# A 32- or 64-row tail of a mixture-of-experts layer on separate column groups of the matrix engine, its sums added up by VectorE

## The chip, the cores and the metric

The kernel runs on one core of a Trainium2 chip. The metric is the device time of one execution in microseconds (us). A core has a matrix engine (PE, with PEld for its weight loads), VectorE (DVE), ScalarE (ACT), GpSimd (POOL) and a sequencer that issues DMAs (SP). PE holds a block of weights of up to 128 rows by 128 columns and streams a second operand past it; the sums land in PSUM, a small memory of eight banks per partition. DVE and ACT read PSUM and write SBUF, and each of the engines runs its own instructions in the order in which they are written.

## What is computed

A causal linear attention over 4 x 768 tokens makes a matrix x of 3072 tokens by 512. Each token then goes to its two best of 8 experts:

```
for e in range(E):
    for k in range(2):
        mask = top2[:, k] == e
        h = np.maximum(x[mask] @ w1[e], 0.0)
        out[mask] += top2_w[mask, k, None] * (h @ w2[e])
```

w1[e] is 512 x 1024 and w2[e] is 1024 x 512. Inputs and outputs are float32. The kernel keeps both operands of a product as a high and a low half in float16 and adds three products (high x high, high x low, low x high).

## The kernel before

The first 230 us are the attention, the gate and the routing, with expert 0 (e = 0) begun as lists of tokens come in. From there the program does one expert after another, e = 1 to 7, and the same engines work ahead on the next expert's weights and tokens.

An expert has tiles of 128 tokens: `tiles(e)` is 7 where the expert has a tail, else 6. `TAILS = (64, 64, 32, 32, 32, 0, 0, 0)` are the rows of the last tile (t = 6) of e = 0 to 7; from e = 1 on the experts are taken in order of how many tokens they have. So there are five tail tiles in the program, two of 64 rows and three of 32.

The first layer (`gemm1`, line 944, with `mm1` and `evac1`) goes by part: the seven tiles are one part of four tiles (512 columns) and one of two tiles and the tail (288 or 320 columns), or 256 columns where there is no tail. For each of 8 blocks f of the hidden size PE makes 12 products into one of four PSUM banks named `pS` (line 955); ACT then writes the high half of the hidden values `ht` (line 961), and DVE the low half (line 965), in two instructions where the part holds a tail. PE can start a fifth block only when DVE has read the first one's bank.

The second layer (`gemm2`, line 988) goes by tile: 24 products of 512 columns into one of two banks `pO` and `pKV` in turn (line 1000), then on DVE one `scalar_tensor_tensor` that scales by the token's gate weight and adds the rows `pv` gathered from the output so far (line 1012), then a scatter by POOL (line 1019). For e = 0 the scaled rows go to `PV[t]` (line 1015).

The tail had a path of its own (lines 1003 to 1011): the high and the low half of `ht` for its n rows lie side by side, so that 16 products with weights of 2n columns give high x high and high x low in rows 0 to n and low x high in rows n to 2n. ACT copies rows n to 2n out of PSUM (line 1008), DVE adds rows 0 to n (line 1009), and the line 1012 or 1015 follows.

The order is written out by hand. In an expert's second layer, behind each tile's `gemm2`, stand the steps for the next expert (lines 1327 to 1343): the scale and split of its first-layer weights (`split_w`, lines 861 and 862), and `trans_rows` for one of its tiles, which is on DVE a block transpose `turned` (line 924), on ACT `xth` (926), on DVE `xtl` (927) and four small ones (929). Behind the tail tile of e = 1, 2 and 3 stands one more `trans_rows`; behind that of e = 4 none, since e = 5 has six tiles. Next come the `gemm1` blocks of the next expert's first part: 288 columns for e + 1 = 2, 3, 4, and 256 for e + 1 = 5.

Of the kernel before, what the change touches and what calls it, by code (L numbers as in the profile page):

```python
# [26 lines left out]
AF = mybir.ActivationFunctionType  # L27
# [12 lines left out]
FB = F // 128  # L40
# [9 lines left out]
FULL = (NT - 1) * TS  # L50
# [44 lines left out]
def size(e, t):  # L95
    return TS if t < NT - 1 else TAILS[e]
# [35 lines left out]
def kernel(  # L132
# [3 lines left out]
    nc = tc.nc  # L136
    MULT, ADD, SUB = OP.mult, OP.add, OP.subtract
# [67 lines left out]
    for i in range(7):  # L205
        n = 1 << i
# [510 lines left out]
    for hp in range(HP):  # L717
        nc.tensor.matmul(PO[0][0][half(side(0, hp)), hp, :], SA[0, 1][half(0), hp, :], qTs[0][half(0), hp, C:],
                         start=True, stop=True)
# [29 lines left out]
    W2 = [[wp.tile([128, 2, DM], HF, name=f"w2{n}{f}") for f in range(FB // 2)] for n in "hl"]  # L749
# [10 lines left out]
    WS, REC, RECQ, PV, HT = {}, {}, {}, [], []  # L760
# [109 lines left out]
    def part_of(t):  # L870

        return min(i for i in range(NG) if t < sum(PARTS0[:i + 1]))
# [95 lines left out]
    def ht(e, part, f, c):  # L968

        at = c.start + (0 if not part else TAILS[e] if c.start >= FULL else LOW)  # L970
        return HT[0][:, f, at:at + c.stop - c.start]
# [3 lines left out]
    winv0 = consts.tile([128, NG], FT, name="winv0")  # L975
# [13 lines left out]
    def gemm2(e, t, then={}):  # L989
        n = size(e, t)  # L990
        cs = slice(t * TS, t * TS + n)
        p = psum.tile([128, DM], FT, name=("pO", "pKV")[next(turn) % 2])
        terms = [(f, a, b) for f in range(FB) for a, b in ((0, 0), (0, 1), (1, 0))]
        o = hp.tile([TS, DM], FT, name="ot", bufs=2) if e else PV[t]
        w, pv = WR[e % 2][:n, t:t + 1], PV[t][:n, :]
        if n == TS:
            for i, (f, a, b) in enumerate(terms):
                if i in then:
                    then[i]()
                nc.tensor.matmul(p, ht(e, a, f, cs), W2[b][f // 2][:, f % 2, :], start=(i == 0),  # L1000
                                 stop=(i == len(terms) - 1))
        else:
            for i in range(2 * FB):
                f, b = i // 2, i % 2
                nc.tensor.matmul(p[:2 * n, :], HT[0][:, f, FULL:FULL + 2 * n], W2[b][f // 2][:, f % 2, :],  # L1005
                                 start=(i == 0), stop=(i == 2 * FB - 1))
            o = o[:n, :]
            nc.scalar.activation(o, p[n:2 * n, :], AF.Copy)
            nc.vector.tensor_add(o, o, p[:n, :])
            p = o  # L1010
        if e:
            nc.vector.scalar_tensor_tensor(o, p, w, pv, op0=MULT, op1=ADD)  # L1012
            scatter_out(e, t, o)
        else:
            nc.vector.tensor_scalar(o, p, w, winv0[:n, part_of(t):part_of(t) + 1], op0=MULT, op1=MULT)

    def scatter_out(e, t, o):
        nc.gpsimd.memset(spacer, 0.0)
        st = nc.gpsimd.indirect_dma_start(  # L1019
            out=out, out_offset=bass.IndirectOffsetOnAxis(ap=REC[e, t], axis=0), in_=o, in_offset=None,  # L1020
            bounds_check=NTOK - 1, oob_is_err=False)
        if t == 0:
            out_st.clear()
        for s in out_st:
            tc.declare_no_dep(st.ins, s.ins, reason="an expert has a token once")
        out_st.append(st)
# [21 lines left out]
    for t in range(NST):  # L1048
# [45 lines left out]
        if 2 * t in GB[1:]:  # L1094
            b = GB.index(2 * t) - 1
# [69 lines left out]
    for i, (t0, n) in enumerate(parts(0)):  # L1165
# [51 lines left out]
        for t in range(t0, t0 + n):  # L1217
            gemm2(0, t, then.get(t, {}))
            if t == 0:
                finish(2, "gated")  # L1220
            if t == 1:
                advance(FILLG)
            if i == 2:
                scatter_out(0, t, PV[t][:size(0, t), :])
            if i == 2:
                if t == t0:
                    scale_w(1, 1)
                for j in range((0, 2, 3)[t - t0], (2, 3, 4)[t - t0]):
                    split_w(1, 1, j)
                for j in range((0, 2, 4)[t - t0], (2, 4, 4)[t - t0]):  # L1230
                    square_w(2, 1, j)
                if t == NT - 1:
                    scale_w(2, 1)
                for j in X1[t]:
                    trans_rows(1, j)
# [62 lines left out]
    for e in range(1, E):  # L1298
# [28 lines left out]
        for t in range(tiles(e)):  # L1327
            gemm2(e, t)
            if e == 1:
                next(ovj, None)  # L1330
            if e + 1 < E:
                if not t:
                    scale_w(1, e + 1)
                elif t < 5:
                    split_w(1, e + 1, t - 1)
                    square_w(2, e + 1, t - 1)
                elif t == 5:
                    scale_w(2, e + 1)
                for j in nxt[t:t + 1]:
                    trans_rows(e + 1, j)  # L1340
                    gather_pieces(2)
                    if e + 2 < E and j < tiles(e + 2):
                        gather_rows(e + 2, j)
    with tc.For_i(0, n_over) as it:
# [34 lines left out]
        for f in range(FB):  # L1379
            p = psum.tile([128, OV], FT, name="pS", bufs=4)  # L1380
            for d in range(DB):
                for i, (a, b) in enumerate(((0, 0), (0, 1), (1, 0))):
                    nc.tensor.matmul(p, W1[a][d][:, f * 128:(f + 1) * 128], xt(b, slice(0, OV))[:, d],
                                     start=(d == 0 and i == 0), stop=(d == DB - 1 and i == 2))
# [3 lines left out]
        p = psum.tile([OV, DM], FT, name="pO")  # L1388
        for f in range(FB):
            for i, (a, b) in enumerate(((0, 0), (0, 1), (1, 0))):  # L1390
                nc.tensor.matmul(p, ht(0, a, f, slice(0, OV)), W2[b][f // 2][:, f % 2, :],
                                 start=(f == 0 and i == 0), stop=(f == FB - 1 and i == 2))
        o = hp.tile([OV, DM], FT, name="ot", bufs=2)
# [30 lines left out]
```

## Time and profile before

| | |
|---|---|
| median of 3 runs | 703.85 us (702.4 to 705.42) |
| the profiled execution | 701.57 us, of which the span of its instructions 699.8 us |
| granted clock of PE, mean over the span | 0.99 |
| PE, DVE, ACT, POOL busy | 673.0, 419.1, 310.4, 361.5 us |

The busy time of an engine says how much it does over the whole span. What a change at one place is worth is read at that place: the timeline there gives for each instruction its start and length, and in brackets how long its engine sat idle before it and what ended that.

### The profile page before, as it was taken

To read this page: it belongs to the slowest core of one execution; us is meant where nothing else is said; L and a number is where in the kernel's file an instruction comes from. 1 tells how busy PE (TensorE), PEld (TensorE's weight loads), DVE (VectorE), ACT (ScalarE), POOL (GpSimd) and SP (SyncE) were. 2 spreads that over 40 slices of the span, in tenths; PEclk is the share of its full clock that TensorE was granted. 3 is DMA by queue.
4 is the path that set the end of the run, shared out by engine and by line. 5 is a ranking of instruction groups with operands and counts; after the bars stand their busy time and mean duration, and the time that the engine had idled before them with its cause. 6 is when DMAs were issued, how large, how long until landed. Compare 5 with 4: busy or idle time off the path is not lost.

```text
span 699.8 us, 15988 instructions
## 1 busy us (share of the span) xinstructions
PE 673.0 (96%) x6033; PEld 403.2 (58%) x6033; DVE 419.1 (60%) x1147; ACT 310.4 (44%) x533; POOL 361.5 (52%) x504
## 2 busy tenths in 40 slices
PE   7899999989989999999999999999999999999994
PEld 5788888775655464464446444644564474456441
DVE  4744988989646656782567257626743782576210
ACT  2267667771127653454335433534353544335100
POOL 4412343313333586578777857775774668331221
PEclk9999999999999999999999999999999999999997
DMA  9999986582383652644355435533462454211110
GB/s 201 238 264 229 259 238 198 186 293 73 99 272 136 188 171 77 183 131 135 118 170 161 115 102 170 161 111 117 134 194 82 146 161 152 69 46 38 59 50 36
DMA packets 94193, 104.33 MB, mean 149 GB/s; under 512 B 41234, under 2 KB 66844, under 8 KB 94112
## 3 DMA queue, kind: packets, MB, share of 16 engines
q1 hardware_dynamic: 79456, 65.73, 33.1%
q0 software_dynamic: 13552, 37.00, 16.8%
q10 hardware_dynamic: 1104, 0.53, 0.5%
q8 instruction: 49, 0.80, 0.5%
q14 instruction: 32, 0.26, 0.1%
HBM read 78.28 MB, written 26.12 MB: 149 GB/s over the span
## 4 chain that ended last, share of the span: by engine, by line
PE 71%; DVE 14%; issue 6%; DMA 4%; ACT 2%; POOL 1%; ACTq 0%; SPq 0%; POOLq 0%; DVEq 0%
PE pS L955 32%; PE pO L1000 13%; PE pKV L1000 12%; PE pO L398 2%; PE pS L386 2%; PE pS L342 2%; DVE at L389 2%; DVE w1l L862 1%; PE pS L464 1%; PE pS L433 1%; PE pS L358 1%; PE pKV L398 1%; DMA xg<-x_tok,recs 1%; PE pO L1005 1%; DMA Mk<-powd 1%
## 5 line engine op out<-in xcount | busy, mean ns | idle before, releaser
L1000 PEld LDWEIGHTS <-ht 128*128 128x128 f16 x1152 | 112.3, 98 | 134.2 <-issue 1.0
L897 POOL DMA_INDIRECT xg<-x_tok,recq x147 | 160.5, 1092 | 44.8 <-issue 41.5
L955 PE MATMUL pS<-xth,w1h 128*128 128x512 f16 (+3 forms) x544 | 175.5, 323 | 3.3 <-DVE ht L965 3.3
L955 PE MATMUL pS<-xtl,w1h 128*128 128x512 f16 (+3 forms) x544 | 175.3, 322 | 1.1 <-DVE wr L942 1.1
L955 PE MATMUL pS<-xth,w1l 128*128 128x512 f16 (+3 forms) x544 | 175.3, 322 | 0.3 <-DVE w1l L862 0.3
L955 PEld LDWEIGHTS <-w1h 128*128 128x128 f16 x1088 | 105.7, 98 | 71.5 <-issue 4.9
L965 DVE SCALAR_TENSOR_TENSOR ht<-pS,ht 128x256 f16<-128x256 f32 (+3 forms) x176 | 74.7, 453 | 105.8 <-ACT ht L961 103.8
L961 ACT ACTIVATE ht<-pS 128x512 f16<-128x512 f32 (+3 forms) x136 | 64.9, 482 | 128.6 <-PE pS L955 118.7
L1000 PE MATMUL pKV<-w2h,ht 128*128 128x512 f16 x384 | 119.1, 381 | 0.0
L1000 PE MATMUL pO<-w2h,ht 128*128 128x512 f16 x384 | 118.1, 379 | 0.0
L1019 POOL DMA_INDIRECT out_dram<-ot,rec x46 | 61.7, 1342 | 102.8 <-DVE ot L1012 71.9
L926 ACT ACTIVATE xth<-turned,xsc 128x512 f16<-128x512 f32 (+1 forms) x39 | 27.2, 697 | 132.1 <-DVE turned L924 132.1
L955 PEld LDWEIGHTS <-w1l 128*128 128x128 f16 x544 | 53.3, 98 | 35.0 <-issue 1.2
L1000 PE MATMUL pKV<-w2l,ht 128*128 128x512 f16 x192 | 73.3, 382 | 0.0
L1000 PE MATMUL pO<-w2l,ht 128*128 128x512 f16 x192 | 72.8, 379 | 0.0
L844 ACT ACTIVATE junk<-wst 128x1024 bf16<-128x1024 f32 x64 | 67.0, 1047 | 0.1
L374 POOL TENSOR_TENSOR kd<-kt,Mk 128x512 f32<-128x512 f32 x24 | 24.8, 1051 | 75.4 <-PE pR L433 52.1
L984 POOL DMA_INDIRECT pv<-out_dram,rec x46 | 46.7, 1015 | 12.8 <-issue 10.2
L927 DVE SCALAR_TENSOR_TENSOR xtl<-turned,xsc,xth 128x512 f16<-128x512 f32 (+1 forms) x39 | 28.2, 722 | 29.9 <-ACT xth L926 29.9
L862 DVE SCALAR_TENSOR_TENSOR w2l<-wst,wsc,w2h 128x1024 f16<-128x1024 f32 x32 | 40.9, 1281 | 4.5 <-ACT w2h L861 4.4
L389 DVE TENSOR_TENSOR at<-pS,Mk 128x512 f32<-128x512 f32 x48 | 29.8, 682 | 22.6 <-PE pS L386 18.1
L862 DVE SCALAR_TENSOR_TENSOR w1l<-wst,wsc,w1h 128x1024 f16<-128x1024 f32 x32 | 40.8, 1276 | 1.2 <-ACT w1h L861 1.2
(255 smaller groups left out, 893.3 us busy)
## 6 DMA issues: line engine op xcount, KB each, us to landing
wst<-in_moe_w_dram SPq DMA_DIRECT2D x36, 512.0 KB, 4.6
wst<-in_moe_w_dram SPq DMA_DIRECT2D x96, 128.0 KB, 2.8
x_tok<-xc SPq DMA_DIRECT2D x24, 272.0 KB, 4.6
kt<-in_k_dram SPq DMA_DIRECT2D x12, 512.0 KB, 4.7
qt<-in_q_dram SPq DMA_DIRECT2D x24, 256.0 KB, 5.4
vt<-in_v_dram SPq DMA_DIRECT2D x12, 512.0 KB, 5.4
out_dram<-zero SPq DMA_DIRECT2D x24, 256.0 KB, 3.2
xg<-x_tok,recq POOLq DMA_INDIRECT x147, 3.3
```

What stands on the lines that cost most here:

```text
L389: nc.vector.tensor_mul(at[:, s], ps[s], mask(s, slice(2 * r, 2 * r + 2), slice(0, C)))
L844: nc.scalar.activation(junk, WS[which, e, j], AF.Square, accum_out=wsq[:, which - 1, j:j + 1])
L862: nc.vector.scalar_tensor_tensor(lo[:, r], st[:, r], s, hi[:, r], op0=MULT, op1=SUB)
L897: nc.gpsimd.indirect_dma_start(out=XG[t][:, g * QW:(g + 1) * QW], out_offset=None, in_=x_tok.rearrange("t (q w) -> (t q) w", w=QW), in_off ...
L926: nc.scalar.activation(hi, raw, AF.Copy, scale=xs)
L927: nc.vector.scalar_tensor_tensor(lo, raw, xs, hi, op0=MULT, op1=SUB)
L955: nc.tensor.matmul(p, W1[a][d][:, fs], xt(b, cs)[:, d], start=(d == 0 and i == 0), stop=(d == DB - 1 and i == 2))
L961: nc.scalar.activation(ht(e, 0, f, cs), p, AF.Relu)
L965: nc.vector.scalar_tensor_tensor(ht(e, 1, f, c), p[:, r], 0.0, ht(e, 0, f, c), op0=OP.max, op1=SUB)
L984: nc.gpsimd.indirect_dma_start(out=PV[t][:size(e, t), :], out_offset=None, in_=out, in_offset=bass.IndirectOffsetOnAxis(ap=REC[e, t], axis=0),
L1000: nc.tensor.matmul(p, ht(e, a, f, cs), W2[b][f // 2][:, f % 2, :], start=(i == 0), stop=(i == len(terms) - 1))
L1019: st = nc.gpsimd.indirect_dma_start(out=out, out_offset=bass.IndirectOffsetOnAxis(ap=REC[e, t], axis=0), in_=o, in_offset=None, bounds_che ...
```

## The change

All 24 products of a tail are now made as for a whole tile, but each has weights of n columns only, and they go in turn to k = 128 / n separate places: product i writes PSUM partitions g n to (g + 1) n with g = i mod k. For 32 rows these are four groups of columns of the array, for 64 rows two. The k partial sums are then added: the first by the instruction that also scales and adds `pv`, each further one by another `scalar_tensor_tensor` on DVE that reads its PSUM rows, scales them and adds the output rows so far. The copy by ACT is gone. For e = 0, which has no `pv`, the gate weight is first scaled in place (a 64x1 instruction), the first sum is a `tensor_scalar`, the second a `scalar_tensor_tensor`.

```diff
-        else:
-            for i in range(2 * FB):
-                f, b = i // 2, i % 2
-                nc.tensor.matmul(p[:2 * n, :], HT[0][:, f, FULL:FULL + 2 * n], W2[b][f // 2][:, f % 2, :],
-                                 start=(i == 0), stop=(i == 2 * FB - 1))
-            o = o[:n, :]
-            nc.scalar.activation(o, p[n:2 * n, :], AF.Copy)
-            nc.vector.tensor_add(o, o, p[:n, :])
-            p = o
...
+        k = 128 // n
+        for i, (f, a, b) in enumerate(terms):
+            g = i % k
+            nc.tensor.matmul(p[g * n:(g + 1) * n, :], ht(e, a, f, slice(FULL, FULL + n)), W2[b][f // 2][:, f % 2, :],
+                             start=(i < k), stop=(i >= len(terms) - k))
+        o = o[:n, :]
+        if e:
+            nc.vector.scalar_tensor_tensor(o, p[:n, :], w, pv, op0=MULT, op1=ADD)
         else:
+            nc.vector.tensor_scalar(w, w, winv0[:n, part_of(t):part_of(t) + 1], None, op0=MULT)
+            nc.vector.tensor_scalar(o, p[:n, :], w, None, op0=MULT)
+        for g in range(1, k):
+            nc.vector.scalar_tensor_tensor(o, p[g * n:(g + 1) * n, :], w, o, op0=MULT, op1=ADD)
         if e:
-            nc.vector.scalar_tensor_tensor(o, p, w, pv, op0=MULT, op1=ADD)
             scatter_out(e, t, o)
```

On DVE at the tail of e = 2, between the two `trans_rows` that stand there (`turned`, `xtl` and `w` are theirs) and the first low halves `ht` of the next expert, the program before has:

```order
L929 SCALAR_TENSOR_TENSOR w_544<-rank,xg_2970 32x7 x4
L1009 TENSOR_TENSOR ot<-ot,pO 32x512
L1012 SCALAR_TENSOR_TENSOR ot<-ot,wr_541,pv_2979 32x512
L924 STREAM_TRANSPOSE turned<-xg_2972 128x512
L927 SCALAR_TENSOR_TENSOR xtl_532<-turned,xsc,xth_531 128x4x128
L929 SCALAR_TENSOR_TENSOR w_544<-rank,xg_2972 32x7 x4
L965 SCALAR_TENSOR_TENSOR ht<-pS,ht 128x256
```

and now, in the same place:

```order
L929 SCALAR_TENSOR_TENSOR w_544<-rank,xg_2970 32x7 x4
L1015 SCALAR_TENSOR_TENSOR ot<-pO,wr_541,pv_2979 32x512
L1020 SCALAR_TENSOR_TENSOR ot<-pO,wr_541,ot 32x512 x3
L924 STREAM_TRANSPOSE turned<-xg_2972 128x512
L927 SCALAR_TENSOR_TENSOR xtl_532<-turned,xsc,xth_531 128x4x128
L929 SCALAR_TENSOR_TENSOR w_544<-rank,xg_2972 32x7 x4
L965 SCALAR_TENSOR_TENSOR ht<-pS,ht 128x256
```

Two instructions of 512 elements became four, at the same point of DVE's order; e = 3 has the same picture. At the tail of e = 0, on DVE, the difference (`w1l` is the low half of the next expert's first-layer weights) is:

```order
 L939 SCALAR_TENSOR_TENSOR w_544<-rank,xg_2974 128x7
-L1009 TENSOR_TENSOR pv_2979<-pv_2979,pO 64x512
-L1015 TENSOR_SCALAR pv_2979<-pv_2979,wr_541,winv_557 64x512
+L1017 TENSOR_SCALAR wr_541<-wr_541,winv_557 64x1
+L1018 TENSOR_SCALAR pv_2979<-pO,wr_541 64x512
+L1020 SCALAR_TENSOR_TENSOR pv_2979<-pO,wr_541,pv_2979 64x512
 L862 SCALAR_TENSOR_TENSOR w1l_522<-wst,wsc,w1h_518 128x1024
```

Two instructions became three here, ahead of the split of the last weight block. At the tail of e = 4, on DVE, where no `trans_rows` follows, the difference is:

```order
 L929 SCALAR_TENSOR_TENSOR w_544<-rank,xg_2972 32x7 x4
-L1009 TENSOR_TENSOR ot<-ot,pO 32x512
-L1012 SCALAR_TENSOR_TENSOR ot<-ot,wr_541,pv_2979 32x512
+L1015 SCALAR_TENSOR_TENSOR ot<-pO,wr_541,pv_2979 32x512
+L1020 SCALAR_TENSOR_TENSOR ot<-pO,wr_541,ot 32x512 x3
 L965 SCALAR_TENSOR_TENSOR ht<-pS,ht 128x256
```

Here the first `ht` of the next expert stands right behind the tail's sums.

## Rows read from the trace of the kernel before

**Rows 1.** Page, part 1: busy us (share of span) xinstructions, by engine.
```profile
PE 673.0 (96%) x6033; PEld 403.2 (58%) x6033; DVE 419.1 (60%) x1147; ACT 310.4 (44%) x533; POOL 361.5 (52%) x504
```

**Rows 2.** Timeline, PE, tail of e=2: start, us, engine, line, op, out<-in, count [idle<-releaser].
```profile
364.53 0.40 PE L1005 MATMUL pO<-w2h,ht 128*64 128x512 f16 x1
...
367.80 0.38 PE L1005 MATMUL pO<-w2l,ht 128*64 128x512 f16 x1
...
368.11 0.30 PE L955 MATMUL pS<-xth,w1h 128*128 128x288 f16 x1
...
374.00 0.29 PE L955 MATMUL pS<-xth,w1h 128*128 128x288 f16 x1
```

**Rows 3.** Timeline, PE, attention: four column groups (L452), then one group (L464).
```profile
56.54 0.64 PE L452 MATMUL pR<-xo,wgn 128*32 128x256 f32 x8
...
57.11 0.45 PE L386 MATMUL pS<-qT,kT 64*64 64x128 f32 x8
...
98.43 1.09 PE L464 MATMUL pS<-identf,xo 128*128 128x128 f32 x8
```

**Rows 4.** Timeline, DVE, from the tail of e=2 into e=3.
```profile
364.64 0.75 DVE L1012 SCALAR_TENSOR_TENSOR ot<-pKV,wr,pv 128x512 f32<-128x512 f32 x1 [0.33 <-PE pL L849]
...
368.83 0.68 DVE L1009 TENSOR_TENSOR ot<-ot,pO 32x512 f32<-32x512 f32 x1
369.54 0.74 DVE L1012 SCALAR_TENSOR_TENSOR ot<-ot,wr,pv 32x512 f32<-32x512 f32 x1
370.21 0.69 DVE L924 STREAM_TRANSPOSE turned<-xg 128x512 f32<-128x512 f32 x1
...
373.22 0.52 DVE L965 SCALAR_TENSOR_TENSOR ht<-pS,ht 128x256 f16<-128x256 f32 x2
...
374.86 0.94 DVE L965 SCALAR_TENSOR_TENSOR ht<-pS,ht 128x256 f16<-128x256 f32 x4
```

**Rows 5.** Timeline, DVE and PE, e=4 begins: first bank read, first bank used again.
```profile
440.61 0.52 DVE L965 SCALAR_TENSOR_TENSOR ht<-pS,ht 128x256 f16<-128x256 f32 x2
...
441.26 0.29 PE L955 MATMUL pS<-xth,w1h 128*128 128x288 f16 x1
```

**Rows 6.** Timeline, DVE and PEld, e=2 begins: the same two places.
```profile
305.99 0.52 DVE L965 SCALAR_TENSOR_TENSOR ht<-pS,ht 128x256 f16<-128x256 f32 x2
...
306.56 0.11 PEld L955 LDWEIGHTS <-w1h 128*128 128x128 f16 x2 [1.23 <-DVE ht L965]
```

**Rows 7.** Timeline, PE and DVE, e=5 begins behind the tail of e=4.
```profile
502.73 0.28 PE L955 MATMUL pS<-xth,w1h 128*128 128x256 f16 x1
...
503.46 0.67 DVE L1009 TENSOR_TENSOR ot<-ot,pO 32x512 f32<-32x512 f32 x1
...
504.84 0.40 DVE L965 SCALAR_TENSOR_TENSOR ht<-pS,ht 128x256 f16<-128x256 f32 x1
...
507.98 0.27 PE L955 MATMUL pS<-xth,w1h 128*128 128x256 f16 x1
```

**Rows 8.** Timeline, DVE and PEld, tail of e=0 and begin of e=1.
```profile
220.25 0.81 DVE L1015 TENSOR_SCALAR pv<-pO,wr,winv 128x512 f32<-128x512 f32 x1 [2.34 <-PE pL L849]
...
220.98 0.15 DVE L485 TENSOR_REDUCE wsum<-pL 128x1 f32<-128x4 f32 x1
...
231.13 0.67 DVE L1009 TENSOR_TENSOR pv<-pv,pO 64x512 f32<-64x512 f32 x1
...
232.30 1.27 DVE L862 SCALAR_TENSOR_TENSOR w1l<-wst,wsc,w1h 128x1024 f16<-128x1024 f32 x1
...
233.62 0.10 PEld L955 LDWEIGHTS <-w1l 128*128 128x128 f16 x1 [0.75 <-DVE w1l L862]
```

**Rows 9.** Windows: PE, PEld, DVE, ACT, POOL busy us (x); granted clock; DMA share, GB/s.
```profile
193.00:197.00 4.00, 1.19 (x11) 0.72 (x8) 1.62 (x4) 1.37 (x2) 1.00 (x1) 1.00 1.04 261
197.00:202.00 5.00, 5.00 (x22) 2.42 (x21) 1.34 (x3) 0.47 (x1) 0.00 (x0) 0.66 1.03 343
303.50:307.00 3.50, 2.58 (x22) 1.83 (x21) 2.62 (x9) 3.29 (x6) 2.58 (x4) 1.00 0.25 62
```

More of the change, by code (lines that the diff above doesn't have):

```diff
@@ L1001, in gemm2 @@
                                  stop=(i == len(terms) - 1))
-        else:
-            for i in range(2 * FB):
-                f, b = i // 2, i % 2
-                nc.tensor.matmul(p[:2 * n, :], HT[0][:, f, FULL:FULL + 2 * n], W2[b][f // 2][:, f % 2, :],
-                                 start=(i == 0), stop=(i == 2 * FB - 1))
-            o = o[:n, :]
-            nc.scalar.activation(o, p[n:2 * n, :], AF.Copy)
-            nc.vector.tensor_add(o, o, p[:n, :])
-            p = o
+            if e:
+                nc.vector.scalar_tensor_tensor(o, p, w, pv, op0=MULT, op1=ADD)
+                scatter_out(e, t, o)
+            else:
+                nc.vector.tensor_scalar(o, p, w, winv0[:n, part_of(t):part_of(t) + 1], op0=MULT, op1=MULT)
+            return
+        k = 128 // n
[4 more added lines that the diff above has]
+        o = o[:n, :]
+        if e:
+            nc.vector.scalar_tensor_tensor(o, p[:n, :], w, pv, op0=MULT, op1=ADD)
+        else:
+            nc.vector.tensor_scalar(w, w, winv0[:n, part_of(t):part_of(t) + 1], None, op0=MULT)
+            nc.vector.tensor_scalar(o, p[:n, :], w, None, op0=MULT)
+        for g in range(1, k):
+            nc.vector.scalar_tensor_tensor(o, p[g * n:(g + 1) * n, :], w, o, op0=MULT, op1=ADD)
         if e:
-            nc.vector.scalar_tensor_tensor(o, p, w, pv, op0=MULT, op1=ADD)
             scatter_out(e, t, o)
-        else:
-            nc.vector.tensor_scalar(o, p, w, winv0[:n, part_of(t):part_of(t) + 1], op0=MULT, op1=MULT)
     def scatter_out(e, t, o):
```

## The prediction, as it was put on record before the changed kernel ran

> **What bounds the kernel now.** I read the busy times first: PE works 673.0 us of the span, 96% [rows 1]. With so little left over, time taken out of PE should shorten the run, unless another engine is late at that very place. I therefore read the timeline of PE around a tail, then that of DVE over the same microseconds, and last the granted clock where PE had stopped.
>
> At the tail of e = 2 the 16 products run from 364.53 to 367.80 at one per 0.218 us, the first product of e = 3 starts at 368.11, and the fifth block of e = 3, which needs the first PSUM bank again, starts at 374.00 [rows 2]. So the tail takes 368.11 - 364.53 = 3.58 us, and four blocks 374.00 - 368.11 = 5.89 us. DVE over the same time is the thing to see: from 364.64, where it last waited for PE, it works off one queue without another wait on PE, comes to the tail's sum only at 368.83, to the transpose at 370.21, and to the first low halves `ht` of e = 3 at 373.22, ending 0.52 us later at 373.74 [rows 4]. That read frees the bank which PE takes again at 374.00. DVE is thus 0.26 us ahead of PE. In e = 4 the read ends at 440.61 + 0.52 = 441.13 and PE takes the bank at 441.26 [rows 5]: 0.13 us. In e = 2 DVE is already late: the read ends at 306.51, and PE, idle for 1.23 us, goes on at 306.56 [rows 6]; 0.05 us is the way from DVE to PE. PE and DVE are level at these places, and the change takes work from PE and gives work to DVE.
>
> **The change part by part: PE.** Do four groups of columns run side by side? In the attention, eight passes with weights of 32 columns, two on each of four groups, take 57.11 - 56.54 = 0.57 us to the next instruction; eight passes of half their length in one group take 1.09 us, so one after another they would be about 2.2 [rows 3]. They do run side by side, 3.8 fold. A 32-row tail is then six rounds, 6 x 0.218 = 1.31 us, and some 0.14 us to enter and leave (0.1 is seen at 368.11): 1.45 instead of 3.58, so 2.13 us less on PE, three times. A 64-row tail has twelve rounds, 2.62 + 0.14 = 2.76 instead of 16 x 0.218 = 3.49, 0.7 us less, twice.
>
> **DVE.** Between two starts, the add took 369.54 - 368.83 = 0.71 us, and the scale-and-add 370.21 - 369.54 = 0.67 us where nothing waits for its result: together 1.38 [rows 4]. The change makes four of the second kind out of these two. Each but the last is followed by one that reads its output, so I give it its length and the 0.03 us that the add shows beyond its own 0.68, with 0.75 as the length where PSUM is read (row of 364.64): 3 x 0.78 + 0.67 = 3.01, and **1.63 us more** per 32-row tail. Bounds: 4 x 0.67 - 1.38 = 1.30 below, and with the 0.81 that a scaled read of PSUM took in e = 0 [rows 8] 3 x 0.84 + 0.81 - 1.38 = 1.95 above. A 64-row tail with `pv` goes from 1.38 to 0.78 + 0.67 = 1.45: 0.07 more. ACT's copy, 0.6 us, lay beside DVE's queue and brings nothing where it goes. POOL's scatter comes 1.6 us later and POOL, 52% busy [rows 1], has the room; if it had not, the gathers behind it would be later by as much.
>
> **Place by place, with the clock as it is.**
> e = 0: DVE's next step is the last weight split `w1l` at 232.30, and PE waits for its end until 233.62. The two instructions took 232.30 - 231.13 = 1.17 us; now a small one (0.15 to 0.2, as the reduce of 220.98), a scaled PSUM read 0.84 and a 0.67 [rows 8]: 1.70. PE goes on 0.53 us later; what it saved it waits. **+0.5** (0.2 to 0.8).
> e = 1: PE already waits for DVE [rows 6]; 0.7 us saved is 0.7 waited, and DVE is 0.07 later. **+0.1**.
> e = 2: the bank is read at 373.74 + 1.63 = 375.37, and PE goes on at 375.42 instead of 374.00: +1.42. One block later it needs the second bank, which DVE reads by 374.86 + half of 0.94 + 1.63 = 376.96 [rows 4], against 375.42 + 5.89 / 4 = 376.89: 0.1 more. **+1.5**.
> e = 3: 441.13 + 1.63 + 0.05 = 442.81 instead of 441.26 [rows 5], and the same 0.1: **+1.65**.
> e = 4: no `trans_rows` lies between. PE starts e = 5 at 502.73 - 2.13 = 500.60 and needs the first bank after 507.98 - 502.73 = 5.25 us, at 505.85; DVE's read comes at 503.46 + 3.01 = 506.47 and ends at 506.87. PE goes on at 506.92 instead of 507.98 [rows 7], and gives back some 0.25 at the second bank, since one weight split (the 1.64 us from 373.22 to 374.86, less one read, in [rows 4]) lies ahead of it. **-0.8** (-1.1 to -0.5).
> Sum: 0.5 + 0.1 + 1.5 + 1.65 - 0.8 = **+3.0 us**. The bounds of DVE's cost, three times over, make it +2.0 to +4.3.
>
> **The clock.** Arriving 2.13 us early and being served 1.6 us late, PE now stops for long: in e = 3 from 374.00 - 2.13 = 371.87 to 375.42, 3.55 us, in e = 4 3.7 us, where it did not stop before. The trace has three stops to compare. Between 193 and 197 us PE was busy for only 1.19 of 4 us, and in the 5 us that followed the granted clock was 0.66 in the mean, half speed (1.2 instead of 2.4 GHz) for 1.7 / 0.5 = 3.4 us, a loss of 5 x 0.34 = 1.7 us; the stop of 0.9 us in 303.5 to 307 left it at 1.00 [rows 9]. A stop of 3.6 us at a stroke is nearer to the first, with 2.8 us of idle time in pieces, so I take it that the clock falls behind both stops. Each costs 1.7 us less the 0.1 that PE then need not wait at the second bank; nothing else hides it, since PE is the bound for the rest of the expert. Part of the slow time may lie in the stop itself, so I take 1.5 each, between 0 and 1.7. In e = 2 the stop grows from 1.2 to 2.0 us, nearer to the one that did nothing.
>
> So **+3.0 + 2 x 1.5 = +6.0 us**. The profiled execution took 701.57 (its span 699.8 and 1.8 around it) and would take 707.6; it lies 2.3 below the median of its three runs, so the forecast for the median is 703.85 + 6.0 = **709.8 us**.
>
> **A rule against this sum.** Rows 3 show the array's four groups at work together. The Trainium skill, "TensorEngine Tiling (Array Packing)", section Theoretical Speedup, gives up to 4x for 32 columns; by that alone the change would be worth the first rival below. The same page, section PSUM Bottleneck, warns that "Tiling speeds up TensorE but not PSUM evacuation", and rows 4 have the evacuation on DVE's queue. The page "TensorE: Matmul & The Clock Gate", Part 3, says that a weight load overlaps running products only where the row groups differ; all groups here use the same 128 rows, which would be the second rival. Rows 2 and 3, where loads and products of the same rows keep full pace, speak against it.
>
> **The rivals.**
> (a) *DVE does not decide, and PE's saving stands*: 3 x 2.13 + 2 x 0.7 = 7.8 us less, 696.0 us, the other side. It needs the extra DVE time to be below 0.26 us in e = 2 and 0.13 in e = 3; four PSUM reads in the time of two are in no row. Against it also e = 0 and e = 1, where PE waits already.
> (b) *The groups do not run side by side*: 24 x 0.218 + 0.1 = 5.3 us per tail, 1.7 more than now. PE then comes to the bank at 375.7, DVE has read it, no stop, no fall of the clock: 3 x 1.7, about 0.7 in e = 1 and 1.2 in e = 0: +7.0, 710.9 us. Against it rows 3.
> (c) *The stops do not slow the clock*: +3.0, 706.9 us. For it: between 193 and 197 us the idle time lay in a longer thin stretch, and the new stops have full work right before and behind them. With one fall of two: +4.5, 708.4 us.
>
> **How the numbers follow.** Both clocks fall 0.45, one 0.18, none 0.17, (b) 0.08, (a) 0.05, and 0.07 for costs of DVE below its bounds, where the time stays within 2 us. What a measurement can tell from no change is about 0.5%, 3.5 us, above 707.4 or below 700.3. Slower: 0.45, most of 0.18 and 0.08, a little of (c), together 0.66. Faster: (a) and a little noise, 0.06. Same: 0.28. Leaving out (a) and the edge cases, the range goes from case (c) less its DVE bound and the spread of the medians, 705.0, to 709.8 with the upper DVE cost (1.3), 1.7 per fall (0.4) and the same spread, 712.5.
>
> **What would show it.** Step by step: the 24 products of a 32-row tail take about 1.45 us (5.3 in (b)). DVE's four sums start with the first still some 4 us behind the last `scale-and-add` of a full tile and take 3.0 us. The fifth block of e = 3 and e = 4 waits 3.5 us for `ht` of line 965, in e = 2 2.0 us, in e = 5 1.1. The granted clock is 0.5 for some 3.4 us shortly after. From e = 5 on nothing changes. Wrong it would be if DVE's sums took under 1.7 us, or if PE did not wait for the low halves at the fifth block.

## The result, and the profile after

The changed kernel takes 710.65 us in the median of seven runs (706.9 to 712.95), the kernel before 703.74 us in seven on the same chip. The medians are 6.9 us apart; the ratio that is estimated from all the runs is 1.0082 (95% interval 1.0056 to 1.0108), which is 5.8 us more (3.9 to 7.6). The ratios given below are such estimates too, so they can differ a little from the quotient of the two medians. The forecast was 709.8 us. The profiled execution is the one of 710.65 us, with a span of 708.8 us at a mean granted clock of 0.986; the kernel before had 699.8 us at 0.990.

PE works less than before and waits more. The busy times of the page after (against [rows 1]), then from its table of groups the first-layer products (busy us, mean ns, idle time before them), then from the table of waits over the whole span what PE waited for (us, times, longest), in the changed kernel and, last, in the kernel before:

```profile
PE 669.2 (94%) x6073; PEld 400.8 (57%) x6073; DVE 425.5 (60%) x1154; ACT 307.4 (43%) x528; POOL 361.5 (51%) x504
```

```profile
L955 PE MATMUL pS<-xth,w1h 128*128 128x512 f16 (+3 forms) x544 | 176.8, 325 | 12.0 <-DVE ht L965 11.9
```

```profile
PE pS L955 <- DVE ht L965: 11.9, 7, 3.5
```

```profile
PE pS L955 <- DVE ht L965: 3.3, 4, 1.2
```

PE is busy for 3.8 us less, though some of its products ran at a lower clock and took longer, and it stands idle 11.9 us ahead of `pS` until DVE has read the bank; in the kernel before it is 3.3 us. The three pieces that answer to [rows 2], [rows 4] and [rows 5] show how. First PE's timeline at the tail of e = 2 and on to the fifth block of e = 3, then that block's first product in e = 4:

```profile
368.56 0.39 PE L1011 MATMUL pO<-w2h,ht 128*32 128x512 f16 x1
...
369.66 0.38 PE L1011 MATMUL pO<-w2h,ht 128*32 128x512 f16 x1
369.97 0.30 PE L955 MATMUL pS<-xth,w1h 128*128 128x288 f16 x1
...
379.41 0.42 PE L955 MATMUL pS<-xth,w1h 128*128 128x288 f16 x1 [3.38 <-DVE ht L965]
...
449.53 0.30 PE L955 MATMUL pS<-xth,w1h 128*128 128x288 f16 x1 [3.52 <-DVE ht L965]
```

The 24 products of the tail take 369.97 - 368.56 = 1.41 us where the 16 took 3.58 [rows 2]. So PE has its gain, and loses it four blocks on: the fifth block waits 3.38 us in e = 3 and 3.52 us in e = 4, where neither waited before. DVE's timeline over the same time:

```profile
368.67 0.75 DVE L1003 SCALAR_TENSOR_TENSOR ot<-pKV,wr,pv 128x512 f32<-128x512 f32 x1 [0.33 <-PE pL L849]
...
372.81 0.74 DVE L1015 SCALAR_TENSOR_TENSOR ot<-pO,wr,pv 32x512 f32<-32x512 f32 x1
373.59 2.31 DVE L1020 SCALAR_TENSOR_TENSOR ot<-pO,wr,ot 32x512 f32<-32x512 f32 x3
375.82 0.69 DVE L924 STREAM_TRANSPOSE turned<-xg 128x512 f32<-128x512 f32 x1
...
378.83 0.52 DVE L965 SCALAR_TENSOR_TENSOR ht<-pS,ht 128x256 f16<-128x256 f32 x2
```

From 372.81 to 375.82 the four sums take 3.01 us, and the transpose, which has nothing to do with them, stands behind. The tail's products were done at about 370.0, but DVE, coming from the last full tile at 368.67, reaches them only at 372.81: making them faster could not bring this forward. The read of the bank ends at 378.83 + 0.52 = 379.35, and PE goes on at 379.41.

The last step is the granted clock. Windows (busy us of PE, PEld, DVE, ACT and POOL with instruction counts, then the granted clock, DMA share, GB/s) over the two stops, the time just after each, and the stop of e = 2, against [rows 9]:

```profile
375.60:379.50 3.90, 0.52 (x5) 0.19 (x3) 2.97 (x10) 2.95 (x6) 2.71 (x3) 0.90 0.04 8
378.70:382.20 3.50, 2.79 (x12) 1.79 (x13) 3.47 (x9) 1.84 (x4) 2.59 (x4) 0.51 0.22 37
445.60:449.60 4.00, 0.48 (x5) 0.17 (x3) 3.07 (x10) 3.06 (x6) 2.83 (x3) 1.00 0.09 21
450.40:453.90 3.50, 3.50 (x17) 2.24 (x15) 3.50 (x11) 1.58 (x3) 2.89 (x3) 0.51 0.68 181
308.50:310.60 2.10, 0.46 (x5) 0.13 (x3) 2.01 (x8) 2.10 (x5) 1.49 (x3) 1.00 0.24 60
```

To each of the two long stops belong 3.5 us at a granted clock of 0.51, that is 1.2 instead of 2.4 GHz, as forecast. In e = 3 they begin within the stop, some 0.7 us before PE goes on at 379.41; in e = 4 they begin 0.9 us behind it. The stop of 2 us in e = 2 (last row) has 1.00. The fall is to be seen in the products themselves, on PE's timeline in e = 4 (starts 0.12 to 0.13 us apart at first, then 0.24):

```profile
450.15 0.29 PE L955 MATMUL pS<-xth,w1l 128*128 128x288 f16 x1
...
450.28 0.29 PE L955 MATMUL pS<-xth,w1h 128*128 128x288 f16 x1
...
450.60 0.45 PE L955 MATMUL pS<-xth,w1l 128*128 128x288 f16 x1
450.84 0.45 PE L955 MATMUL pS<-xth,w1h 128*128 128x288 f16 x1
```

### The profile page after: what moved, and what is told of

It reads as the page before. It is cut to its first block, busy times and chain, and to the rows that moved or that the text cites. A ratio compares the mean times of both kernels' runs of the same rounds, so it can differ in the third digit from the quotient of the medians.

```text
span 708.8 us, 16059 instructions
## 1 busy us (share of the span) xinstructions
PE 669.2 (94%) x6073; PEld 400.8 (57%) x6073; DVE 425.5 (60%) x1154; ACT 307.4 (43%) x528; POOL 361.5 (51%) x504
## 4 chain that ended last, share of the span: by engine, by line
PE 68%; DVE 15%; issue 7%; DMA 4%; ACT 2%; POOL 1%; SPq 0%; DVEq 0%; POOLq 0%; ACTq 0%
PE pS L955 30%; PE pO L1000 12%; PE pKV L1000 12%; PE pO L398 2%; PE pS L386 2%; PE pS L342 2%; DVE w1l L862 1%; DVE at L389 1%; PE pS L433 1%; PE pS L464 1%; PE pS L358 1%; DMA xg<-x_tok,recs 1%; DVE ht L965 1%; PE pKV L398 1%; DMA Mk<-powd 1%
## 5 line engine op out<-in xcount | busy, mean ns | idle before, releaser
L955 PE MATMUL pS<-xth,w1h 128*128 128x512 f16 (+3 forms) x544 | 176.8, 325 | 12.0 <-DVE ht L965 11.9
```

What stands on the lines that cost most here:

```text
L955: nc.tensor.matmul(p, W1[a][d][:, fs], xt(b, cs)[:, d], start=(d == 0 and i == 0), stop=(d == DB - 1 and i == 2))
```

## The account, place by place

The spans of the two profiled executions differ by 9.0 us, but 3.4 of these lie ahead of the first tail, in what the change does not touch: the second-layer products of the last tiles of e = 0, the tail among them, begin at 214.86 us before and 218.24 after, and in the experiments anywhere from there to 222.6. So I compare stretches of PE's timeline that begin there: from the first of those products to the first product of the fifth block of e = 1, from there to the same product of e = 2, and so on to e = 5, and from there to the last product. The stretch "to e=3", for example, holds the tail of e = 2, which the prediction calls the place e = 2. Each figure is the stretch's length less that of the kernel before. For e = 3 to e = 4, for example, 449.53 - 379.41 = 70.12 after against 441.26 - 374.00 = 67.26 before: +2.86. The table holds the experiments as well, which are described below.

| us, against before | to e=1 | to e=2 | to e=3 | to e=4 | to e=5 | to end | sum | medians |
|---|---|---|---|---|---|---|---|---|
| after | +0.59 | +0.06 | +1.39 | +2.86 | +0.60 | +0.21 | +5.7 | +6.9 |
| dve_only | 0 | 0 | +1.22 | +1.51 | +0.07 | 0 | +2.8 | +3.0 |
| first_sum | -0.19 | -0.73 | -0.94 | -0.64 | -2.09 | 0 | -4.6 | -5.2 |
| warm | +0.59 | +0.07 | +1.39 | +1.68 | -0.92 | +0.21 | +3.0 | +3.0 |
| later_cols | -0.44 | -1.45 | -1.62 | -1.42 | -2.09 | 0 | -7.0 | -8.4, -7.2 |
| later_old_b | -0.44 | -1.08 | -0.16 | 0 | -0.09 | 0 | -1.8 | -2.0 |
| two_groups_b | +0.59 | +0.08 | -0.18 | +0.11 | -0.80 | 0 | -0.2 | -0.7 |
| later_both_b | -0.44 | -1.74 | -2.32 | -2.16 | -2.26 | 0 | -8.9 | -9.5 |

The last column is the difference of the medians, with both kernels on the same chip. It follows the sum within 1.4 us in every row, and the largest gap is in a kernel with four runs, whose interval is 7 us wide. So what the kernels differ by lies in these stretches, and the stretches tell where.

## The experiments

The theory: DVE's queue decides. Its additional sums delay the read of the PSUM bank, PE waits for that read, and the two stops lower the clock. The rivals: the groups of columns cost something of their own on PE; DVE's sums are harmless, and something else came with the change; the clock has no part in it.

**dve_only: DVE's additional work alone.** On the kernel before, with PE's 16 products as they were, two more reads of PSUM that add nothing:

```
-            p = o
+            p, bank_ = o, p
         if e:
             nc.vector.scalar_tensor_tensor(o, p, w, pv, op0=MULT, op1=ADD)
+            if n == 32:
+                for _ in range(2):
+                    nc.vector.scalar_tensor_tensor(o, bank_[:n, :], 0.0, o, op0=MULT, op1=ADD)
```

> The kernel before with nothing changed on PE: behind the sum of each 32-row tail stand two more scale-and-add instructions of DVE (times zero, so the sums stay the same). Theory (DVE's queue sets the end): 2 x 0.78 = 1.56 us later at the first bank read; e = 2 waits 1.35, e = 3 1.5, e = 4 nothing since there DVE is 2.7 us ahead; the second bank adds 0.1 each: +3.0 us, about 706.7; the stops are under 1.6 us and the clock stays up. Rival (the column groups themselves, the switch of the array, are what costs): no column groups here, so no change, 703.7.

Measured: 706.6 us (10 runs) against 703.63 (21 runs), ratio 1.0042 (1.001 to 1.0075). DVE's timeline at the tail of e = 2, then PE at the fifth block of e = 3, then two windows around the fifth blocks of e = 3 and e = 4:

```profile
373.94 0.68 DVE L1009 TENSOR_TENSOR ot<-ot,pO 32x512 f32<-32x512 f32 x1
...
375.43 1.39 DVE L1015 SCALAR_TENSOR_TENSOR ot<-pO,ot 32x512 f32<-32x512 f32 x2
376.75 0.69 DVE L924 STREAM_TRANSPOSE turned<-xg 128x512 f32<-128x512 f32 x1
...
379.75 0.52 DVE L965 SCALAR_TENSOR_TENSOR ht<-pS,ht 128x256 f16<-128x256 f32 x2
```

```profile
380.33 0.30 PE L955 MATMUL pS<-xth,w1h 128*128 128x288 f16 x1 [1.06 <-DVE ht L965]
```

```profile
370.00:390.00 20.00, 18.94 (x129) 12.34 (x127) 16.27 (x42) 9.89 (x17) 14.02 (x14) 1.00 0.43 134
440.00:460.00 20.00, 18.82 (x128) 12.26 (x127) 15.67 (x37) 10.76 (x18) 14.39 (x13) 1.00 0.49 143
```

The two additional instructions delay DVE by 1.4 us: from the add of line 1009 to the transpose it takes 376.75 - 373.94 = 2.81 us instead of 1.38 [rows 4]. The expectation had 1.56. PE's fifth blocks come 1.22 and 1.51 us later; in e = 3 that is the delay less the slack of 0.2 us (0.26, of which 0.05 is the way from DVE to PE). DVE's work alone, without a column group, slows the kernel: there is next to no slack between DVE and PE. PE does not come early here, so it stops for 1.06 us only, and the clock holds at 1.00.

**first_sum: the column groups without the additional sums.** On the changed kernel, the sums behind the first are left out, for all tails:

```
-        for g in range(1, k):
+        for g in range(1, 1):
```

> The changed kernel without the further sums: only the first of the four (or two) partial sums is added, the others are left out. PE does what it does in the changed kernel, DVE has one instruction per tail. Theory: DVE comes 0.7 us earlier to the first bank than in the kernel before and PE's saving is paid out up to that: e = 0 -0.2, e = 1 -0.7, e = 2 -0.9, e = 3 -0.8, e = 4 -2.1, together -4.7 us, about 699; stops of 1.2 us, no fall of the clock. Rival (column groups cost): as slow as the changed kernel less nothing, 707 to 711.

Measured: 698.4 us (7 runs), ratio 0.9918 (0.9893 to 0.9943). DVE's timeline at the tail of e = 2, and PE's waits from 235 to 520 us:

```profile
375.62 0.74 DVE L1015 SCALAR_TENSOR_TENSOR ot<-pO,wr,pv 32x512 f32<-32x512 f32 x1
376.29 0.69 DVE L924 STREAM_TRANSPOSE turned<-xg 128x512 f32<-128x512 f32 x1
```

```profile
PE pS L955 <- DVE ht L965: 3.1, 3, 1.2
```

Now the tail takes DVE 0.67 us instead of 1.38, and the start of e = 3 comes 0.94 us earlier; from the rows of before, 0.71 less on DVE gives 373.74 - 0.71 + 0.05 = 373.08 instead of 374.00, or 0.92. In e = 5, where DVE now has time to spare, all of PE's gain appears: -2.09 of the 2.17 that 3.58 - 1.41 make. The groups bring what they should, and the sums decide whether it is kept.

**warm: the same stops without an idle PE.** On the changed kernel, 18 products of zeros behind the tails of e = 2 and e = 3, that is ahead of the two long stops:

```
             gemm2(e, t)
+            if t == NT - 1 and size(e, t) == 32 and e < 4:
+                keep_warm(18)
```

> The changed kernel with 18 dummy products of 384 columns on PE behind the tails of e = 2 and e = 3, 2.9 us that lie where PE would wait for DVE. Theory: PE comes to the fifth block some 0.7 us ahead of DVE instead of 3.6, the places stay as late as in the changed kernel, but the clock does not fall there: the changed kernel's time less 2 x 1.5, that is +3.0 against the kernel before, about 706.8. Rival (the clock falls because the products of 32 columns use little of the array, not because of the stop): it still falls, time 710 or above.

Measured: 706.59 us (10 runs), ratio 1.0045 (1.0016 to 1.0073). PE's timeline, and windows around the same two places:

```profile
368.69 3.10 PE L183 MATMUL pR<-zero 128*128 128x384 bf16 x18
...
378.13 0.30 PE L955 MATMUL pS<-xth,w1h 128*128 128x288 f16 x1 [0.46 <-DVE ht L965]
```

```profile
360.00:395.00 35.00, 34.54 (x225) 19.71 (x223) 24.07 (x57) 15.64 (x27) 25.58 (x27) 1.00 0.53 152
430.00:465.00 35.00, 34.41 (x224) 19.65 (x223) 24.09 (x57) 14.86 (x26) 25.50 (x27) 1.00 0.49 146
```

Up to the fifth block of e = 3 warm is as late as the changed kernel (+1.39 in both), since DVE is as late; but PE's stop is 0.46 us instead of 3.38, and the granted clock stays at 1.00. The rival falls with it, for the products of 32 columns are all there. Two places part the two kernels: to e = 4 2.86 - 1.68 = 1.18 us, and to e = 5 0.60 + 0.92 = 1.52. So the two falls cost 2.7 us. In the medians, useless work that fills the stops made the kernel faster by 4 us, but the intervals of the two ratios overlap; the 2.7 us of the two places are the safer figure. It does not bring the kernel back to before.

**later_cols: the column groups, with the sums out of the way.** On the changed kernel, the tail's sums and its scatter are put behind the first part of the next expert's first layer, where nobody waits for DVE:

```
+        def sums():
             if e:
                 nc.vector.scalar_tensor_tensor(o, p[:n, :], w, pv, op0=MULT, op1=ADD)
...
+            scatter_out(e, t, o)
+        later.append(sums)
...
                 gather_pieces(1)
+            if i == 0 and later:
+                later.pop()()
```

> The changed kernel with the tail's sums and its scatter moved back on DVE: for e = 1 to 4 behind the first part of the next expert's first layer, for e = 0 behind the transposes of the last two tiles of e = 1. Theory: PE's saving is paid out up to the next bound: e = 0 -0.85 (ACT's split is next), e = 1 -1.4, e = 2 -1.6 and e = 3 -1.5 (DVE 1.38 us earlier at the first bank), e = 4 -2.1: -7.4 us, about 696.3, clock up. Rival (column groups cost): 707 to 711. If the moved sums collide with the second part's reads, part of the gain is given back there.

Measured: 695.23 us (4 runs), ratio 0.9869 (0.9819 to 0.992). DVE's timeline into e = 3, PE at its fifth block, and PE's waits from 230 to 520 us:

```profile
369.69 0.68 DVE L929 SCALAR_TENSOR_TENSOR w<-rank,xg 32x7 f32<-32x7 f32 x4
370.40 0.52 DVE L965 SCALAR_TENSOR_TENSOR ht<-pS,ht 128x256 f16<-128x256 f32 x2
...
378.87 0.73 DVE L1019 SCALAR_TENSOR_TENSOR ot<-pO,wr,pv 32x512 f32<-32x512 f32 x1
```

```profile
370.98 0.30 PE L955 MATMUL pS<-xth,w1h 128*128 128x288 f16 x1 [0.38 <-DVE ht L965]
```

```profile
PE pS L955 <- DVE ht L965: 0.8, 2, 0.4
```

The same sums, as many as in the changed kernel, begin 8.5 us behind the read of the bank instead of ahead of it, and PE's waits for that read shrink to 0.8 us. What remains is the last transpose of the next expert's tokens, still ahead of the read. At e = 0 the expectation missed: -0.44 us instead of -0.85, which is the whole difference between -7.0 and the expected -7.4. PE waits there for the sums of squares of the next weights, which ACT makes (line 844), ahead of a product that adds them up:

```profile
230.33 0.17 PE L849 MATMUL pL<-wsq,ones 128*128 128x4 bf16 x1 [0.80 <-ACT junk L844]
```

The changed kernel has the same wait of 0.8 us, and then the one for `w1l`.

**later_old, two_groups and later_both, on a chip that cannot be compared.** Three more kernels, described at their repetition below, ran on another chip.

> The kernel before, its 16 products of a tail unchanged, with only the tail's copy, sums and scatter moved back as in later_cols. It parts what the order gave there from what the column groups gave. Theory: e = 0 -0.4 (PE comes to the weight split later than in later_cols), e = 1 -1.1 (PE's own work is next), e = 2 to 4 nothing, since PE was the bound there: -1.5 us, about 702.1; later_cols is 5.5 us faster. Rival (the order alone made later_cols fast): about 696.

> The changed kernel with two groups for the 32-row tails too, so that DVE has two sums per tail as before the change, while PE makes a tail in 2.8 us instead of 3.6. Theory (what decides is the number of sums on DVE): e = 0 +0.55, e = 1 +0.05, e = 2 -0.15, e = 3 0, e = 4 -0.75, no long stop, clock up: -0.3 us, about 703.3, no change that can be measured. Rival (column groups cost, whatever DVE does): 706 or more.

> later_cols with the transpose of one more tile, which stands behind the tail of e = 1, 2 and 3, moved back behind the fourth block of the next expert. Theory: DVE is then over 3 us ahead at the first bank, so that PE gets the rest of its saving: e = 1 0.35, e = 2 and e = 3 0.55 more each, about 1.4 us faster than later_cols, 694. Against it: the moved transpose may delay the reads behind it, and POOL's gathers that go with it start 5 us later; then equal to later_cols.

Measured there: 747.31, 720.65 and 725.87 us, with the kernel before itself at 718.94 (711.85 to 731.16). PE's waits in later_old over the whole span have this row, of waits that end with nothing that the profile shows:

```profile
PE pS L955 <- issue: 25.2, 46, 1.8
```

It is 25.2 us in later_old, 13.2 in later_both and 5.9 in two_groups, and the disturbance is larger than what is to be told apart. The expectations of the repetitions take these waits for a lack of instructions on PE; no run shows that. All three are repeated, with later_cols beside them, on a chip where the kernel before took 703.98 us (22 runs).

**later_old_b: the sums out of the way, without the column groups.** On the kernel before, the tail's copy, add and scale are put where later_cols has its sums:

```
-            nc.scalar.activation(o, p[n:2 * n, :], AF.Copy)
-            nc.vector.tensor_add(o, o, p[:n, :])
-            p = o
+            def sums():
+                nc.scalar.activation(o, p[n:2 * n, :], AF.Copy)
+                nc.vector.tensor_add(o, o, p[:n, :])
...
+            later.append(sums)
+            return
```

> later_old once more, on a chip on which PE gets its instructions in time. Theory: -1.5 us against the kernel before, about 702.1; later_cols is 5.5 us faster. Rival (the order alone made later_cols fast): about 696.

Measured: 702.01 us (10 runs), ratio 0.9975 (0.995 to 1.0). The move alone is worth 1.8 us by places, nearly all in the stretches to e = 1 and e = 2, where PE waited for DVE before. In those to e = 3, 4 and 5 it is worth 0.16, 0 and 0.09: PE and DVE were level there in the kernel before, and a shorter queue on DVE alone gives nothing while PE's tail keeps its length.

**two_groups_b: half as many groups, half as many additional sums.** On the changed kernel, two groups of 32 columns in place of four:

```
-        k = 128 // n
+        k = 2
```

> two_groups once more, on a chip on which PE gets its instructions in time. Theory: e = 0 +0.55, e = 1 +0.05, e = 2 -0.15, e = 3 0, e = 4 -0.75, no long stop, clock up: -0.3 us, about 703.3, no change that can be measured. Rival (column groups cost, whatever DVE does): 706 or more.

Measured: 703.31 us (10 runs), ratio 0.9995 (0.9967 to 1.0023). DVE's timeline at the tail of e = 2, and PE's waits from 235 to 520 us:

```profile
372.85 0.74 DVE L1015 SCALAR_TENSOR_TENSOR ot<-pO,wr,pv 32x512 f32<-32x512 f32 x1
373.62 0.74 DVE L1020 SCALAR_TENSOR_TENSOR ot<-pO,wr,ot 32x512 f32<-32x512 f32 x1
374.29 0.69 DVE L924 STREAM_TRANSPOSE turned<-xg 128x512 f32<-128x512 f32 x1
```

```profile
PE pS L955 <- DVE ht L965: 2.8, 3, 1.7
```

Two sums take 1.44 us, about the 1.38 of before, and the stretches to e = 3 and e = 4 are within 0.2 us of it, though PE's tail is shorter (twelve rounds of products for sixteen). The number of sums sets the time there, not the number of products.

**later_both_b: the transpose out of the way as well.** On later_cols, the next expert's last `trans_rows`, with the gathers that follow it, is put behind the fourth block of that expert:

```
+                if turn_later and i == 0 and f == 3:
+                    turn_one(*turn_later.pop())
...
+                    if t == NT - 1:
+                        turn_later.append((e + 1, j))
+                    else:
+                        turn_one(e + 1, j)
```

> later_both once more, on a chip on which PE gets its instructions in time. Theory: about 1.4 us faster than later_cols, 694; if the moved transpose or POOL's later gathers delay what is behind them, equal to later_cols.

> later_cols once more, beside the other orders on one chip. Theory: 695 to 696, 5.5 us below later_old_b, about 1.4 above later_both_b.

Measured: later_both_b 694.45 us (7 runs, 691.98 to 700.4), ratio 0.9876 (0.984 to 0.9911), and later_cols_b 696.8 us (4 runs), ratio 0.9888 (0.9825 to 0.995). DVE's timeline of later_both_b into e = 3, then its busy times:

```profile
367.13 0.70 DVE L929 SCALAR_TENSOR_TENSOR w<-rank,xg 32x7 f32<-32x7 f32 x4
367.87 0.52 DVE L965 SCALAR_TENSOR_TENSOR ht<-pS,ht 128x256 f16<-128x256 f32 x2
...
372.73 0.70 DVE L924 STREAM_TRANSPOSE turned<-xg 128x512 f32<-128x512 f32 x1
```

```profile
PE 663.7 (96%) x6073; PEld 398.6 (58%) x6073; DVE 424.6 (61%) x1154; ACT 307.2 (44%) x528; POOL 356.9 (52%) x504
```

From 235 to 520 us PE no longer waits for DVE at any product of `pS`. With as much work on every engine as in the changed kernel (DVE 424.6 us against 425.5), by places it is 8.9 + 5.7 = 14.6 us faster than that; only the order on DVE differs, and with it the stops. It has the lowest median of all, and its interval lies clear of the kernel before. Against later_cols it is ahead by 1.9 us by places (1.4 expected); the intervals of the two ratios overlap. Between later_old_b and later_cols_b, which differ only in how the tail is made and have its sums at the same late place, lie 5.2 us, by places and by medians: that is what the column groups are worth there.

## Why the prediction was right

**PE's tail.** Forecast 1.45 us, measured 1.41. Rival (b), that the groups would run one after another (5.3 us), falls with that row: 24 products in the time of six and a half. That each group loads its own weights on the same 128 rows costs at most the 0.10 us by which 1.41 exceeds six rounds of 0.218. The rule of the Trainium skill, "TensorE: Matmul & The Clock Gate", Part 3, that a load overlaps products only where the row groups differ, would by itself speak for rival (b); the measurement of 1.41 us decides against it here.

**DVE's tail.** Forecast 3 x 0.78 + 0.67 = 3.01, measured 3.01 (372.81 to 375.82). The step that carried it was to price a sum by whether the next instruction reads its result: from start to start, three take 0.77 to 0.78 and the last 0.68. dve_only's sums, which take a constant instead of `wr`, show the same step at a lower level, 0.71 and 0.61, so that kernel is a little cheaper on DVE than the change.

**Places with the clock as it is.** The answer is warm, which has the stops' lateness without the falls: e = 0 forecast +0.5, measured +0.59 (from 234.50 to 236.26 us, where the three instructions of the tail stand ahead of `w1l`, 1.76 us against 1.17 in [rows 8]); e = 1 +0.1 and +0.07; e = 2 and e = 3 together +3.15 and 1.39 + 1.68 = +3.07; e = 4 -0.8 and -0.92 + 0.21 = -0.7, of which the 0.21 is given back at the second bank, behind the fifth block, as reckoned (0.25). Sum +3.0, as forecast. The stops came as the last part of the prediction asked: 3.38 and 3.52 us (3.5), in e = 2 1.95 (2.0), in e = 5 1.01 (1.1). The last two, PE's weight load in e = 2 and the product in e = 5, against [rows 6] and [rows 7]:

```profile
310.59 0.11 PEld L955 LDWEIGHTS <-w1h 128*128 128x128 f16 x2 [1.95 <-DVE ht L965]
```

```profile
516.85 0.27 PE L955 MATMUL pS<-xth,w1h 128*128 128x256 f16 x1 [1.01 <-DVE ht L965]
```

**The clock.** Forecast 2 x 1.5 = 3.0 us, measured 1.18 + 1.52 = 2.7. The fall of e = 3 is the cheaper one. The windows place it: of the 3.9 us from 375.60 on, 0.10 of the clock is missing, so at half speed some 0.8 us lie inside, and PE went on only at 379.41. Part of the slow time fell into the stop, which the prediction allowed for. In e = 4 the window of the stop shows 1.00, and the fall at 450.4 lies wholly in work. Why one fall begins earlier than the other stays open. Rival (c) falls by these windows and by warm. The expectation that a stop of 2 us would leave the clock alone holds too: 1.00 in the window from 308.50. That the clock would fall at all was taken from a single example [rows 9], so this step could well have failed. The falls are seen in one traced execution of the changed kernel. The mean granted clocks of its seven runs (0.981 to 0.991, against 0.985 to 0.994 in 21 runs of the kernel before) agree with them, but do not show them for every run.

**The sum.** +5.7 us by places against the forecast +6.0, the difference being the 0.3 of the clock. The ratio gives +5.8 (3.9 to 7.6), the medians +6.9. The prediction took the profiled execution of before, 2.3 us below its median, and moved the median by the same amount; that works where the spread from run to run falls on both kernels alike, and much of it lies ahead of the first tail, where the last part of e = 0 begins anywhere from 214.9 to 222.6 us. That the median came out only 0.9 us from the forecast is luck in part, since single runs of the changed kernel lie 6 us apart. Two slips in the prediction changed nothing: DVE's upper bound, three times over, gives 3.0 + 3 x (1.95 - 1.63) = +4.0 and not +4.3, and of the "three stops to compare" it names only two.

**Rival (a).** That DVE does not decide and all of PE's gain stands (-7.8 us) fell for the change as it was made. Its size was about right: later_cols has -7.0 and later_both_b -8.9, of which the sums' move alone is 1.8. What was missing was not a property of the array but the order on DVE. The sentence of the Trainium skill, "TensorEngine Tiling (Array Packing)", PSUM Bottleneck, that tiling leaves the evacuation of PSUM as slow as it was agrees with the trace (3.01 us of sums behind 1.41 us of products).

Left open: what PE waited for on the one chip. That the later_ kernels gain up to 1.4 us more in the medians than by places is within their intervals.

## What to carry to other kernels

Work taken from the bounding engine stays gained only if the engine that frees its buffers is ahead at that very place; compare the two queues there, to the tenth of a microsecond, before you trade products for sums. Sums that nobody waits for belong behind the reads that free a bank; with that order, and one transpose moved as well, the same change went from 6.9 us slower to 9.5 us faster in the medians. And where the bounding engine will stop for as long as here (3.4 us and more), add the price of its slower clock: here 2.7 of 5.7 us.

## What the runs showed of the hardware beyond what was expected

- The granted clock fell to 0.5 at both stops of 3.4 to 3.5 us, with full work right before and behind them, and stayed at 1.00 at the stop of 2 us. In the one example ahead of the prediction [rows 9] PE had been thinly busy for longer, so this was an inference then. The fall that began within the stop cost less (1.18 us) than the one behind it (1.52).
- Products of zeros that kept PE busy held the clock at 1.00 and repaid 2.7 us, with no later start of the work behind them: PE took up the fifth block within 0.01 us of where the changed kernel did, reckoned from the same product of e = 2.
- A scale-and-add out of PSUM takes DVE 0.74 us by its row for 32 rows (above) and 0.75 for 128 [rows 4]. The groups' sums are thus no cheaper for being small: each group of columns more costs a whole one.
- On one chip PE stood still ahead of `pS` for 5.9 us (two_groups) and 13.2 us (later_both) in waits that end with nothing the profile shows; the same two programs have no such wait there on another chip (two_groups_b, later_both_b). The cause stays open.
